# A second fold of the sequence DFT, and zero-padded column tiles for the last 64 keys, in a fused attention and Fourier-mixing kernel

## Chip, cores, metric

One core of one Trainium2 chip. The metric is the device time of one execution in microseconds (us); the medians below are over several runs. The profile of a kernel is one execution taken by the hardware profiler; its span is some 2 us shorter than the timed run.

## The reference

Threshold attention over 8 batches, 8 heads, 576 positions, 64 columns a head; its output, as (batch, 576, 512), is mixed by a two-dimensional DFT of which the real part is kept, and goes through a normalised two-layer network. All in fp32.

```python
scores = scale * np.matmul(q, k.transpose(0, 1, 3, 2))
thresh = np.max(scores, axis=-1, keepdims=True) - tau
scores = np.where(scores >= thresh, scores, -1e9)
attn = softmax(scores)                      # written out in the reference
x = heads_side_by_side(np.matmul(attn, v))  # (8, 576, 512)

X = np.fft.fft(np.fft.fft(x, axis=1), axis=2)
u = x + np.real(X)
un = (u - mean(u)) / np.sqrt(var(u) + 1e-6)
out = u + np.maximum(un @ w_ch1, 0.0) @ w_ch2   # 512 -> 2048 -> 512
```

## The kernel before

Heads go two at a time: 32 pairs, four to a batch, five query tiles to a pair. Every pair ends in `weighted_values`. Its last chunk of 64 keys is done in 64x64 tiles of the array. Then GpSimd folds x by the symmetry of the cosine and the sine, x(s) + x(576-s) and x(s) - x(576-s).

```python
    for c in range(4):
        for j in range(2):
            nc.tensor.matmul(pv[64*j : 64*j+64, 0:HALF], vt[:, 2*c+j, :],
                             e_t[:, 4*j+c, cols], start=(c == 0), stop=False, ...)
    for j in range(2):
        hp = slice(64 * j, 64 * j + 64)
        nc.tensor.matmul(pv[hp, 0:HALF], vt[hp, 8, :], ends[hp, 0, cols],
                         start=False, stop=True, ...)
    # ... x = pv times the reciprocal sums, on VectorE; then
    nc.gpsimd.tensor_copy(f[:, p, 0:KH:HALF], x[:, 0:KH:HALF])
    nc.gpsimd.tensor_tensor(out=f[:, p, 1:HALF], in0=up, in1=down, op=ALU.add)
    nc.gpsimd.tensor_tensor(out=f[:, p, KH:S], in0=up, in1=down, op=ALU.subtract)
```

After a batch's fourth pair its mixing starts: sums over the four pairs on VectorE (`s01` first), the DFT over the columns (`py`), and the DFT over the sequence, five calls of

```python
    def over_seq(y, table, rows, cols, m):
        pa = ps.tile([128, 512], FP32, tag="mm", name="pa")
        for u in range(3):                      # rows: 128, 128 and 33 or 31
            n = rows[u][1]
            nc.tensor.matmul(pa[0:m, 0:KH], y[0:n, u, cols], table[0:n, u, :],   # KH = 289
                             start=(u == 0), stop=(u == 2))
```

The network (`ph`, `po`) of earlier batches is woven between the attention steps of later ones. The order of instructions on each engine is fixed when the kernel is built, from estimated times: an engine that meets an instruction whose input is late stands still, whatever stands behind it.

Of the kernel before, what the change touches and what calls it, by code (L numbers as in the profile page):

```python
# [47 lines left out]
def kernel(  # L48
# [12 lines left out]
    nc = tc.nc  # L61
# [21 lines left out]
    ps = ctx.enter_context(tc.tile_pool(name="ps", bufs=2, space=bass.MemoryType.PSUM))  # L83


    loaded = {}
# [6 lines left out]
    def load_pair(n):  # L93
# [3 lines left out]
        kt = sb.tile([128, NT, 2, D], FP32, tag="k", bufs=1, name="k_in")  # L97
        vt = sb.tile([128, 9, D], FP32, tag="v", name="v_in")
        for j, h in enumerate(hs):
# [14 lines left out]
        nc.sync.dma_start(out=kt[64:128, 0:4, 1, :], in_=rows[:, 0])  # L114
        nc.sync.dma_start(out=kt[0:64, 1:5, 1, :], in_=rows[:, 1])

        for j, h in enumerate(hs):
            nc.sync.dma_start(
                out=vt[:, j:8:2, :], in_=v[b, h, 0:512, :].rearrange("(t p) d -> p t d", p=128)
            )  # L120
            nc.sync.dma_start(out=vt[64 * j : 64 * j + 64, 8, :], in_=v[b, h, 512:576, :])
        loaded[n] = (qt, kt, vt)

    load_pair(0)


# [30 lines left out]

    E_ROWS = [(0, 128), (128, 128), (256, KH - 256)]
    O_ROWS = [(0, 128), (128, 128), (256, HALF - 1 - 256)]
    seq_c = const.tile([128, 3, KH], FP32, name="seq_c")  # L160
    seq_s = const.tile([128, 3, KH], FP32, name="seq_s")
    for u in range(3):
        r, n = E_ROWS[u]
        nc.gpsimd.dma_start(out=seq_c[0:n, u, :], in_=dft_seq[r : r + n, 0:KH])
        r, n = O_ROWS[u]
        nc.gpsimd.dma_start(out=seq_s[0:n, u, :], in_=dft_seq[1 + r : 1 + r + n, KH : 2 * KH])

# [22 lines left out]

    load_dim()

    w1 = [const.tile([128, HID], FP32, name=f"w1_{c}") for c in range(ND)]
# [8 lines left out]
    u_t = const.tile([128, ND, RING], FP32, name="u_t")  # L202
    y_e = const.tile([128, 3, EH], FP32, name="y_e")
    y_o = const.tile([128, 3, 256], FP32, name="y_o")


# [78 lines left out]
    xs = {}  # L285
    folds = {}

    def prep_pair(n):

        qt, kt, vt = loaded.pop(n)  # L290
        ts = []
        for src, tag in ((qt, "qT"), (kt, "kT")):
            pt = ps.tile([128, 1024], FP32, tag="wide", bufs=3, name="pt")
            for t in range(NT):
                m = ROWS[t]
                nc.tensor.transpose(  # L296
                    pt[:, 128 * t : 128 * t + m], src[0:m, t, :, :], ident[0:m, 0:m]
                )
            dst = sb.tile([128, S], FP32, tag=tag, name=tag)
            if tag == "qT":  # L300
                nc.vector.tensor_scalar(
                    out=dst[:, :], in0=pt[:, 0:S], scalar1=q_scale[:, :], scalar2=None, op0=ALU.mult
                )
            else:
                nc.scalar.copy(dst[:, :], pt[:, 0:S])
            ts.append(dst)
        heads[n] = (ts[0], ts[1], vt)
        if n + 1 < B * NPAIR:
            load_pair(n + 1)
# [49 lines left out]
    def transposed_weights(i):  # L359
# [3 lines left out]
        if t == 0:  # L363
# [5 lines left out]
            if PAIRS[n % NPAIR] % 2:  # L369

                vt = sb.tile([128, 9, D], FP32, tag="vr", bufs=1, name="v_rev")
                src = heads[n][2]
# [23 lines left out]
    def weighted_values(n):  # L396
# [3 lines left out]
        if n % NPAIR == 0:  # L400
            xs[b] = [None] * NPAIR
            folds[b] = sb.tile([128, ND, S], FP32, tag="fold", bufs=1, name="fold")
        x = sb.tile([128, S], FP32, tag=f"x{p}", bufs=1, name=f"x{p}")
        for h in range(2):
            cols = slice(HALF * h, HALF * (h + 1))
            pv = ps.tile([128, 512], FP32, tag="mm", name="pv")
            for c in range(4):
                for j in range(2):
                    nc.tensor.matmul(  # L409
                        pv[64 * j : 64 * j + 64, 0:HALF], vt[:, 2 * c + j, :],  # L410
                        e_t[:, 4 * j + c, cols], start=(c == 0), stop=False,
                        skip_group_check=True,
                    )
            for j in range(2):
                hp = slice(64 * j, 64 * j + 64)
                nc.tensor.matmul(  # L416
                    pv[hp, 0:HALF], vt[hp, 8, :], ends[hp, 0, cols],
                    start=False, stop=True, skip_group_check=True,
                )
            nc.vector.tensor_tensor(  # L420
                out=x[:, cols], in0=pv[:, 0:HALF], in1=ends[:, 1, cols], op=ALU.mult
            )
        if p % 2:

            swap = sb.tile([2, S], FP32, tag="swap", bufs=1, name="swap")
            for j in range(2):
                nc.sync.dma_start(out=swap[j : j + 1, :], in_=x[64 * j : 64 * j + 1, :])
            for j in range(2):
                nc.sync.dma_start(out=x[64 * j : 64 * j + 1, :], in_=swap[1 - j : 2 - j, :])
        xs[b][p] = x  # L430
        up, down = x[:, 1:HALF], _reversed(x[:, HALF + 1 : S])
        f = folds[b]
        nc.gpsimd.tensor_copy(f[:, p, 0:KH:HALF], x[:, 0:KH:HALF])
        nc.gpsimd.tensor_tensor(out=f[:, p, 1:HALF], in0=up, in1=down, op=ALU.add)
        nc.gpsimd.tensor_tensor(out=f[:, p, KH:S], in0=up, in1=down, op=ALU.subtract)

    MIX = 4 * (3 * 5 * 128 + 5 * 3 * KH)

# [3 lines left out]
    def mixing(b):  # L442
        x = xs.pop(b)
        f = folds.pop(b)
        slot = slice(S * (b % 2), S * (b % 2) + S)



        E, O = slice(0, KH), slice(KH, S)
        s01 = sb.tile([128, 2, S], FP32, tag="tmp", bufs=1, name="s01")  # L450
        nc.vector.tensor_tensor(out=s01[:, :, :], in0=f[:, 0:2, :], in1=f[:, 2:4, :], op=ALU.add)
# [15 lines left out]
        SIN = ((0, 0, 128), (3, 128, 256))  # L467
        for u in range(3):
            for odd in range(2):
                r, n = (O_ROWS if odd else E_ROWS)[u]  # L470
                py = ps.tile([128, 512], FP32, tag="mm", name="py")
                table, first = (dim_s, 0) if odd else (dim_c, 1)
                for c, c0, c1 in SIN if odd else COS:
                    nc.tensor.matmul(  # L474
                        py[0:n, c0:c1], f[:, c, odd * KH + r : odd * KH + r + n],
                        table[:, c0:c1], start=True, stop=True, skip_group_check=True,
# [9 lines left out]

        def over_seq(y, table, rows, cols, m):
            pa = ps.tile([128, 512], FP32, tag="mm", name="pa")
            for u in range(3):
                n = rows[u][1]  # L490
                nc.tensor.matmul(  # L491
                    pa[0:m, 0:KH], y[0:n, u, cols], table[0:n, u, :],
                    start=(u == 0), stop=(u == 2),
                )
            return pa

        for t in range(2):
            cols = slice(128 * t, 128 * t + 128)
            tmp = sb.tile([128, 3, KH], FP32, tag="tmp", bufs=1, name="tmp")
            low, high, sin = (tmp[:, c, :] for c in range(3))  # L500
            pb = over_seq(y_o, seq_s, O_ROWS, cols, 128)
            nc.scalar.copy(sin, pb[:, 0:KH])
            yield MIX / 11
            pa = over_seq(y_e, seq_c, E_ROWS, cols, 128)

# [18 lines left out]
            if t == 1:  # L524

                pa = over_seq(y_e, seq_c, E_ROWS, slice(256, 257), 1)
                nc.scalar.copy(sin[0:1, :], pa[0:1, 0:KH])
# [100 lines left out]
    for i in range(total + 1):  # L628
# [9 lines left out]
        if i > 0 and t == 0:  # L638
            weighted_values(n - 1)
        for _ in itertools.islice(chunks, 2):  # L640
            pass
# [61 lines left out]
```

## Time and profile before

| | before |
|---|---|
| time, median of the first 3 runs | 1922.66 us (1922.33 to 1924.85) |
| TensorE busy | 96% of the span |
| VectorE, ScalarE, GpSimd busy | 45%, 32%, 12% |
| granted TensorE clock, mean | 0.973 |
| half-clock stretches after 250 us | none until the last microsecond |

The lines, and how they are read, stand with the prediction.

### The profile page before, as it was taken

To read this page: it belongs to the slowest core of one execution; us is meant where nothing else is said; L and a number is where in the kernel's file an instruction comes from. 1 tells how busy PE (TensorE), PEld (TensorE's weight loads), DVE (VectorE), ACT (ScalarE), POOL (GpSimd) and SP (SyncE) were. 2 spreads that over 40 slices of the span, in tenths; PEclk is the share of its full clock that TensorE was granted. 3 is DMA by queue.
4 is the path that set the end of the run, shared out by engine and by line. 5 is a ranking of instruction groups with operands and counts; after the bars stand their busy time and mean duration, and the time that the engine had idled before them with its cause. 6 is when DMAs were issued, how large, how long until landed. Compare 5 with 4: busy or idle time off the path is not lost.

```text
span 1923.0 us, 20963 instructions
## 1 busy us (share of the span) xinstructions
PE 1845.8 (96%) x7840; PEld 992.8 (52%) x7840; DVE 870.4 (45%) x2015; ACT 612.5 (32%) x1110; POOL 236.9 (12%) x438
## 2 busy tenths in 40 slices
PE   6777899999999999999999999999999999999999
PEld 3444555455455455545555455545545445545454
DVE  6998555534333544544334444544434355431010
ACT  3555434333123334323223234322323233421010
POOL 3433110110000110011000020002000020001000
PEclk8876899999999999999999999999999999999999
DMA  5432100100000110100000010101000001000000
GB/s 150 129 113 77 32 19 14 37 24 13 18 22 22 30 25 14 31 24 13 18 24 19 18 31 13 31 24 25 13 23 19 24 19 25 1 11 6 11 6 16
DMA packets 129701, 56.97 MB, mean 30 GB/s; under 512 B 120677, under 2 KB 120678, under 8 KB 129600
## 3 DMA queue, kind: packets, MB, share of 16 engines
q1 hardware_dynamic: 129232, 54.71, 10.5%
q8 instruction: 62, 1.02, 0.2%
q0 software_dynamic: 368, 0.93, 0.2%
q14 instruction: 39, 0.32, 0.1%
HBM read 46.02 MB, written 9.44 MB: 29 GB/s over the span
## 4 chain that ended last, share of the span: by engine, by line
PE 86%; DVE 9%; ACT 1%; POOL 1%; issue 1%; SPq 0%; DMA 0%; DVEq 0%; ACTq 0%
PE po L582 26%; PE ph L561 25%; PE sc L319 10%; PE pv L409 7%; PE pw L387 6%; PE pa L491 3%; PE pt L296 2%; PE pv L416 2%; DVE neg L332 2%; PE py L474 2%; DVE e L345 2%; DVE stage L241 1%; PE pe L392 1%; PE pe L393 1%; DVE w L229 1%
## 5 line engine op out<-in xcount | busy, mean ns | idle before, releaser
L582 PE MATMUL po<-w,h 128*128 128x512 f32 x1152 | 537.3, 603 | 0.0
L561 PE MATMUL ph<-u_t,w 128*128 128x384 f32 x1536 | 528.7, 493 | 5.4 <-DVE h L569 3.3
L342 ACT ACTIVATE e<-sc,neg 128x576 f32<-128x576 f32 (+1 forms) x320 | 229.3, 740 | 582.3 <-DVE neg L332 579.4
L561 PEld LDWEIGHTS ph<-u_t,w 128*128 128x128 f32 x1536 | 280.7, 190 | 207.3 <-issue 22.5
L332 DVE TENSOR_REDUCE neg<-sc 128x1 f32<-128x576 f32 (+1 forms) x320 | 229.8, 750 | 328.3 <-PE sc L319 328.0
L582 PEld LDWEIGHTS po<-w,h 128*128 128x128 f32 x1152 | 204.4, 190 | 229.8 <-issue 224.4
L319 PE MATMUL sc<-kT,qT 64*128 64x288 f32 (+1 forms) x1280 | 260.2, 450 | 36.3 <-ACT e_t L390 19.1
L345 DVE SCALAR_TENSOR_TENSOR e<-sc,thr,e 128x576 f32<-128x576 f32 (+1 forms) x320 | 250.9, 814 | 30.3 <-ACT e L342 13.0
L319 PEld LDWEIGHTS sc<-kT,qT 64*128 64x128 f32 (+1 forms) x1280 | 128.5, 183 | 168.3 <-issue 99.6
L390 ACT COPY e_t<-pw 128x1024 f32<-128x1024 f32 (+1 forms) x160 | 148.3, 927 | 160.1 <-PE pw L387 154.8
L354 POOL COPY rec<-den 128x128 f32<-128x128 f32 (+1 forms) x160 | 50.0, 313 | 1105.0 <-DVE den L352 933.8
L387 PEld LDWEIGHTS pw<-ident,e 128*128 128x128 f32 (+1 forms) x1280 | 141.7, 146 | 72.3 <-issue 55.5
L387 PE MATMUL pw<-ident,e 128*128 128x128 f32 (+1 forms) x1280 | 168.7, 275 | 0.1
L567 ACT ACTIVATE h<-ph 128x384 f32<-128x384 f32 x96 | 47.2, 492 | 314.7 <-PE ph L561 314.7
L569 DVE TENSOR_SCALAR h<-ph 128x384 f32<-128x384 f32 x96 | 53.4, 556 | 185.1 <-PE ph L561 184.9
L420 DVE TENSOR_TENSOR x<-pv,ends 128x288 f32<-128x288 f32 x64 | 29.3, 457 | 192.1 <-PE pv L416 175.3
L589 DVE SCALAR_TENSOR_TENSOR u<-po,rstd,u 128x512 f32<-128x512 f32 x36 | 27.0, 750 | 157.1 <-PE po L582 157.1
L409 PE MATMUL pv<-e_t,v_in 128*64 128x288 f32 x512 | 72.5, 420 | 0.0
L409 PE MATMUL pv<-e_t,v_rev 128*64 128x288 f32 x512 | 71.8, 420 | 0.3
L394 ACT COPY ends<-pe 128x256 f32<-128x256 f32 (+1 forms) x160 | 57.1, 357 | 3.2 <-PE pe L393 3.2
L409 PEld LDWEIGHTS pv<-e_t,v_in 128*64 128x64 f32 x512 | 35.0, 139 | 38.0 <-issue 10.8
L409 PEld LDWEIGHTS pv<-e_t,v_rev 128*64 128x64 f32 x512 | 34.8, 139 | 37.6 <-issue 11.6
(98 smaller groups left out, 1266.4 us busy)
## 6 DMA issues: line engine op xcount, KB each, us to landing
stage<-in_moe_w_ch_dram SPq DMA_DIRECT2D x32, 512.0 KB, 4.0
out_dram<-u SPq DMA_DIRECT2D x36, 256.0 KB, 2.0
q_in<-in_q_dram SPq DMA_DIRECT2D x64, 128.0 KB, 2.4
v_in<-in_v_dram SPq DMA_DIRECT2D x64, 128.0 KB, 2.3
k_in<-in_k_dram SPq DMA_DIRECT2D x32, 128.0 KB, 2.4
k_in<-in_k_dram SPq DMA_DIRECT2D x64, 64.0 KB, 2.3
q_in<-in_q_dram SPq DMA_DIRECT2D x64, 16.0 KB, 2.2
k_in<-in_k_dram SPq DMA_DIRECT2D x64, 16.0 KB, 2.1
```

Of the source, the lines that this page charges most:

```text
L319: nc.tensor.matmul(sc[j][0:m, c, 0:HALF], qT[hp, 128 * t : 128 * t + m], kT[hp, HALF * c : HALF * (c + 1)], start=True, stop=True,)
L332: nc.vector.tensor_reduce(out=neg[0:m, j : j + 1], in_=sc[j][0:m, :, 0:HALF], axis=AXIS_XY, op=ALU.max, negate=True,)
L342: nc.scalar.activation(out=ej, in_=sc[j][0:m, :, 0:HALF], func=ACT.Exp, bias=neg[0:m, j : j + 1], scale=1.0)
L345: nc.vector.scalar_tensor_tensor(out=ej, in0=sc[j][0:m, :, 0:HALF], scalar=thr[0:m, j : j + 1], in1=ej, op0=ALU.is_ge, op1=ALU.mult, accum ...
L387: nc.tensor.transpose(pw[:, 4 * j + c, 0:m], e[0:m, c0 : c0 + 128], ident[0:m, 0:m])
L390: nc.scalar.copy(e_t[:, :, qs], pw[:, :, 0:m])
L394: nc.scalar.copy(ends[:, :, qs], pe[:, 0:2, 0:m])
L409: nc.tensor.matmul(pv[64 * j : 64 * j + 64, 0:HALF], vt[:, 2 * c + j, :], e_t[:, 4 * j + c, cols], start=(c == 0), stop=False, skip_group_ ...
L491: nc.tensor.matmul(pa[0:m, 0:KH], y[0:n, u, cols], table[0:n, u, :], start=(u == 0), stop=(u == 2),)
L561: nc.tensor.matmul(ph[:, 0:GT], w1[c][:, 128 * j : 128 * (j + 1)], u_t[:, c, c0 : c0 + GT], start=(c == 0), stop=(c == ND - 1),)
L569: nc.vector.tensor_relu(ht, ph[:, 0:GT])
L582: nc.tensor.matmul(po[:, :], hT[j // 4][:, j % 4, 128 * t : 128 * (t + 1)], w2[j][:, :], start=(j == 0), stop=(j == NJ - 1),)
```

## The change

Its intent is less TensorE work. The folded sequence is folded again about its quarter: even frequencies need only one half-sum, odd ones the other. Each `over_seq` becomes four matmuls of 145 or 144 columns with full 128-row chunks, which write every second column of the PSUM tile. The last 64 keys become a fifth chunk of the same 128x64 column tiles, with v padded by zero rows.

```diff
-            for c in range(4):
+            for c in range(5):
                 for j in range(2):
                     nc.tensor.matmul(
                         pv[64 * j : 64 * j + 64, 0:HALF], vt[:, 2 * c + j, :],
-                        e_t[:, 4 * j + c, cols], start=(c == 0), stop=False,
+                        e_t[:, 4 * j + c, cols] if c < 4 else ends[:, 0, cols],
+                        start=(c == 0), stop=(c == 4), skip_group_check=True,
...
-        nc.gpsimd.tensor_copy(f[:, p, 0:KH:HALF], x[:, 0:KH:HALF])
-        nc.gpsimd.tensor_tensor(out=f[:, p, 1:HALF], in0=up, in1=down, op=ALU.add)
-        nc.gpsimd.tensor_tensor(out=f[:, p, KH:S], in0=up, in1=down, op=ALU.subtract)
+        for c, op in enumerate((ALU.add, ALU.subtract)):
+            nc.gpsimd.tensor_tensor(out=half[:, c, 1:HALF], in0=up, in1=down, op=op)
+        for c, c0, op in (
+            (0, 0, ALU.add), (0, 161, ALU.subtract), (1, FW, ALU.subtract), (1, FW + 161, ALU.add)
+        ):
+            nc.gpsimd.tensor_tensor(
+                out=f[:, p, c0 : c0 + mid - 1], in0=half[:, c, 1:mid],
+                in1=_reversed(half[:, c, mid + 1 : HALF]), op=op,
+            )
+        # ... and two sums of two columns each, on GpSimd
...
+        for parity, u, table, extra in ((0, 0, seq_even, seq_xe), (1, 2, seq_odd, seq_xo)):
+            at = pa[0:m, parity:KH:2]
+            nc.tensor.matmul(at, y[:, u, cols], table[:, odd, :], start=True, stop=False, ...)
+            nc.tensor.matmul(at, y[:, 1, cols], extra[:, odd, :], start=False, stop=True, ...)
...
     load_pair(0)
+    load_v(0)
+    load_v(1)
     # ... the sequence tables: raw rows through the buffers of tag "e", SyncE's queue,
     #     and strided copies on GpSimd, in place of six direct loads on GpSimd's queue
```

More of the change, by code (lines that the diff above doesn't have):

```diff
@@ L83 @@
     ps = ctx.enter_context(tc.tile_pool(name="ps", bufs=2, space=bass.MemoryType.PSUM))
+    y_e = const.tile([128, 3, EH], FP32, name="y_e")
+    y_o = const.tile([128, 3, 256], FP32, name="y_o")
+    FW = 304
+    f = const.tile([128, ND, 2 * FW], FP32, name="f")
+    nc.gpsimd.memset(f[:, :, :], 0.0)
+    nc.vector.memset(y_e[:, 1, :], 0.0)
+    nc.vector.memset(y_o[:, 1, :], 0.0)
+    v_in = [const.tile([128, 10, D], FP32, name=f"v_in{u}") for u in range(2)]
+    for u in range(2):
+        for j in range(2):
+            nc.gpsimd.memset(v_in[u][64 - 64 * j : 128 - 64 * j, 8 + j, :], 0.0)
     loaded = {}
@@ L97, in load_pair @@
         kt = sb.tile([128, NT, 2, D], FP32, tag="k", bufs=1, name="k_in")
-        vt = sb.tile([128, 9, D], FP32, tag="v", name="v_in")
         for j, h in enumerate(hs):
@@ L115, in load_pair, with load_v @@
         nc.sync.dma_start(out=kt[0:64, 1:5, 1, :], in_=rows[:, 1])
-        for j, h in enumerate(hs):
+        loaded[n] = (qt, kt)
+    def load_v(n):
+        b, p = n // NPAIR, PAIRS[n % NPAIR]
+        vt = v_in[n % 2]
+        for j in range(2):
+            h = 2 * p + (j + p) % 2
             nc.sync.dma_start(
@@ L120, in load_pair @@
             )
-            nc.sync.dma_start(out=vt[64 * j : 64 * j + 64, 8, :], in_=v[b, h, 512:576, :])
-        loaded[n] = (qt, kt, vt)
+            nc.sync.dma_start(out=vt[64 * j : 64 * j + 64, 8 + j, :], in_=v[b, h, 512:576, :])
     load_pair(0)
+    load_v(0)
+    load_v(1)
     ident = const.tile([128, 128], FP32, name="ident")
@@ L154, with load_seq @@
     nc.vector.tensor_tensor(out=thr_off[:], in0=tau_pos[:], in1=below[:], op=ALU.add)
-    E_ROWS = [(0, 128), (128, 128), (256, KH - 256)]
-    O_ROWS = [(0, 128), (128, 128), (256, HALF - 1 - 256)]
-    seq_c = const.tile([128, 3, KH], FP32, name="seq_c")
-    seq_s = const.tile([128, 3, KH], FP32, name="seq_s")
-    for u in range(3):
-        r, n = E_ROWS[u]
-        nc.gpsimd.dma_start(out=seq_c[0:n, u, :], in_=dft_seq[r : r + n, 0:KH])
-        r, n = O_ROWS[u]
-        nc.gpsimd.dma_start(out=seq_s[0:n, u, :], in_=dft_seq[1 + r : 1 + r + n, KH : 2 * KH])
+    NE, NO = KH // 2 + 1, KH // 2
+    seq_even = const.tile([128, 2, NE], FP32, name="seq_even")
+    seq_odd = const.tile([128, 2, NO], FP32, name="seq_odd")
+    seq_xe = const.tile([128, 2, NE], FP32, name="seq_xe")
+    seq_xo = const.tile([128, 2, NO], FP32, name="seq_xo")
+    def load_seq():
+        nc.gpsimd.memset(seq_xe[:, :, :], 0.0)
+        nc.gpsimd.memset(seq_xo[:, :, :], 0.0)
+        for pieces, dst, parity, parts in (
+            (((0, 1, 128),), seq_even, 0, ((0, 128),)),
+            (((0, 16, 128),), seq_odd, 1, ((0, 128),)),
+            (((0, 129, 16), (16, 0, 1)), seq_xe, 0, ((0, 17),)),
+            (((32, 0, 16),), seq_xo, 1, ((32, 16),)),
+        ):
+            raw = sb.tile([128, 2 * KH], FP32, tag="e", name="seq_raw")
+            for p, r, n in pieces:
+                nc.sync.dma_start(out=raw[p : p + n, :], in_=dft_seq[r : r + n, :])
+            if dst is seq_xo:
+                nc.sync.dma_start(out=raw[32:33, KH : 2 * KH], in_=dft_seq[144:145, KH : 2 * KH])
+            for p, n in parts:
+                for c in range(2):
+                    nc.gpsimd.tensor_copy(
+                        dst[p : p + n, c, :], raw[p : p + n, KH * c + parity : KH * (c + 1) : 2]
+                    )
     dim_c = const.tile([128, 1 + 256], FP32, name="dim_c")
@@ L191 @@
     load_dim()
+    load_seq()
     w1 = [const.tile([128, HID], FP32, name=f"w1_{c}") for c in range(ND)]
@@ L202 @@
     u_t = const.tile([128, ND, RING], FP32, name="u_t")
-    y_e = const.tile([128, 3, EH], FP32, name="y_e")
-    y_o = const.tile([128, 3, 256], FP32, name="y_o")
     ones = const.tile([128, 128], FP32, name="ones")
@@ L285 @@
     xs = {}
-    folds = {}
     def prep_pair(n):
-        qt, kt, vt = loaded.pop(n)
+        qt, kt = loaded.pop(n)
         ts = []
@@ L306, in prep_pair @@
             ts.append(dst)
-        heads[n] = (ts[0], ts[1], vt)
+        heads[n] = (ts[0], ts[1], v_in[n % 2])
         if n + 1 < B * NPAIR:
@@ L369, in transposed_weights @@
             if PAIRS[n % NPAIR] % 2:
-                vt = sb.tile([128, 9, D], FP32, tag="vr", bufs=1, name="v_rev")
+                vt = sb.tile([128, 10, D], FP32, tag="vr", bufs=1, name="v_rev")
                 src = heads[n][2]
@@ L401, in weighted_values @@
             xs[b] = [None] * NPAIR
-            folds[b] = sb.tile([128, ND, S], FP32, tag="fold", bufs=1, name="fold")
         x = sb.tile([128, S], FP32, tag=f"x{p}", bufs=1, name=f"x{p}")
@@ L410, in weighted_values @@
                         pv[64 * j : 64 * j + 64, 0:HALF], vt[:, 2 * c + j, :],
-                        e_t[:, 4 * j + c, cols], start=(c == 0), stop=False,
-                        skip_group_check=True,
-                    )
-            for j in range(2):
-                hp = slice(64 * j, 64 * j + 64)
-                nc.tensor.matmul(
-                    pv[hp, 0:HALF], vt[hp, 8, :], ends[hp, 0, cols],
-                    start=False, stop=True, skip_group_check=True,
-                )
+                        e_t[:, 4 * j + c, cols] if c < 4 else ends[:, 0, cols],
+                        start=(c == 0), stop=(c == 4), skip_group_check=True,
+                    )
             nc.vector.tensor_tensor(
@@ L423, in weighted_values @@
         if p % 2:
-            swap = sb.tile([2, S], FP32, tag="swap", bufs=1, name="swap")
+            swap = sb.tile([2, S], FP32, tag="half", bufs=1, name="swap")
             for j in range(2):
@@ L430, in weighted_values @@
         xs[b][p] = x
+        half = sb.tile([128, 2, HALF], FP32, tag="half", bufs=1, name="half")
         up, down = x[:, 1:HALF], _reversed(x[:, HALF + 1 : S])
-        f = folds[b]
-        nc.gpsimd.tensor_copy(f[:, p, 0:KH:HALF], x[:, 0:KH:HALF])
-        nc.gpsimd.tensor_tensor(out=f[:, p, 1:HALF], in0=up, in1=down, op=ALU.add)
-        nc.gpsimd.tensor_tensor(out=f[:, p, KH:S], in0=up, in1=down, op=ALU.subtract)
-    MIX = 4 * (3 * 5 * 128 + 5 * 3 * KH)
+        mid = S // 4
+        for c, op in enumerate((ALU.add, ALU.subtract)):
+            nc.gpsimd.tensor_tensor(out=half[:, c, 1:HALF], in0=up, in1=down, op=op)
+        for c, c0, op in (
+            (0, 0, ALU.add), (0, 161, ALU.subtract), (1, FW, ALU.subtract), (1, FW + 161, ALU.add)
+        ):
+            nc.gpsimd.tensor_tensor(
+                out=f[:, p, c0 : c0 + mid - 1], in0=half[:, c, 1:mid],
+                in1=_reversed(half[:, c, mid + 1 : HALF]), op=op,
+            )
+        nc.gpsimd.tensor_tensor(
+            out=f[:, p, mid - 1 : mid + 1], in0=_stepped(x, mid, -mid, 2),
+            in1=_stepped(x, 3 * mid, -mid, 2), op=ALU.add,
+        )
+        nc.gpsimd.tensor_tensor(
+            out=_stepped(f[:, p, :], 160, FW, 2), in0=_stepped(x, 0, mid, 2),
+            in1=_stepped(x, HALF, mid, 2), op=ALU.subtract,
+        )
+    MIX = 4 * (3 * 5 * 128 + 5 * 2 * KH)
     def mixing(b):
         x = xs.pop(b)
-        f = folds.pop(b)
         slot = slice(S * (b % 2), S * (b % 2) + S)
-        E, O = slice(0, KH), slice(KH, S)
-        s01 = sb.tile([128, 2, S], FP32, tag="tmp", bufs=1, name="s01")
+        E, O = slice(0, FW), slice(FW, 2 * FW)
+        s01 = sb.tile([128, 2, 2 * FW], FP32, tag="tmp", bufs=1, name="s01")
         nc.vector.tensor_tensor(out=s01[:, :, :], in0=f[:, 0:2, :], in1=f[:, 2:4, :], op=ALU.add)
@@ L467, in mixing @@
         SIN = ((0, 0, 128), (3, 128, 256))
-        for u in range(3):
+        for u, r, n in ((0, 0, 128), (1, 128, 48), (2, 176, 128)):
             for odd in range(2):
-                r, n = (O_ROWS if odd else E_ROWS)[u]
                 py = ps.tile([128, 512], FP32, tag="mm", name="py")
@@ L474, in mixing @@
                     nc.tensor.matmul(
-                        py[0:n, c0:c1], f[:, c, odd * KH + r : odd * KH + r + n],
+                        py[0:n, c0:c1], f[:, c, odd * FW + r : odd * FW + r + n],
                         table[:, c0:c1], start=True, stop=True, skip_group_check=True,
@@ L485, in mixing, with over_seq @@
                 yield MIX / 11
-        def over_seq(y, table, rows, cols, m):
+        def over_seq(y, odd, cols, m):
             pa = ps.tile([128, 512], FP32, tag="mm", name="pa")
-            for u in range(3):
-                n = rows[u][1]
+            for parity, u, table, extra in ((0, 0, seq_even, seq_xe), (1, 2, seq_odd, seq_xo)):
+                at = pa[0:m, parity:KH:2]
                 nc.tensor.matmul(
-                    pa[0:m, 0:KH], y[0:n, u, cols], table[0:n, u, :],
-                    start=(u == 0), stop=(u == 2),
+                    at, y[:, u, cols], table[:, odd, :], start=True, stop=False,
+                    skip_group_check=True,
+                )
+                nc.tensor.matmul(
+                    at, y[:, 1, cols], extra[:, odd, :], start=False, stop=True,
+                    skip_group_check=True,
                 )
@@ L500, in mixing @@
             low, high, sin = (tmp[:, c, :] for c in range(3))
-            pb = over_seq(y_o, seq_s, O_ROWS, cols, 128)
+            pb = over_seq(y_o, 1, cols, 128)
             nc.scalar.copy(sin, pb[:, 0:KH])
             yield MIX / 11
-            pa = over_seq(y_e, seq_c, E_ROWS, cols, 128)
+            pa = over_seq(y_e, 0, cols, 128)
             nc.vector.tensor_tensor(out=low, in0=pa[:, 0:KH], in1=sin, op=ALU.subtract)
@@ L524, in mixing @@
             if t == 1:
-                pa = over_seq(y_e, seq_c, E_ROWS, slice(256, 257), 1)
+                pa = over_seq(y_e, 0, slice(256, 257), 1)
                 nc.scalar.copy(sin[0:1, :], pa[0:1, 0:KH])
@@ L639 @@
             weighted_values(n - 1)
+            if n + 1 < B * NPAIR:
+                load_v(n + 1)
         for _ in itertools.islice(chunks, 2):
```

## The prediction

> **What bounds the kernel now.** I read the page's busy table and forty slices first, then the table by stage, then the groups of the lines that the diff touches, then the order of time around single uses of them. The busy table, the slices and the chain of work that ended last:
>
> ```profile
> PE 1845.8 (96%) x7840; PEld 992.8 (52%) x7840; DVE 870.4 (45%) x2015; ACT 612.5 (32%) x1110; POOL 236.9 (12%) x438
> ...
> PE   6777899999999999999999999999999999999999
> ...
> DVE  6998555534333544544334444544434355431010
> ...
> PE 86%; DVE 9%; ACT 1%; POOL 1%; issue 1%; SPq 0%; DMA 0%; DVEq 0%; ACTq 0%
> ```
>
> The table by stage (PE, PEld, DVE, ACT, POOL busy, then granted clock, DMA share, GB/s):
>
> ```profile
> 100.00:150.00 50.00, 37.76 (x149) 21.01 (x149) 45.41 (x92) 25.16 (x42) 18.50 (x18) 0.70 0.35 113
> 600.00:1000.00 400.00, 395.65 (x1739) 210.28 (x1738) 175.43 (x413) 126.74 (x226) 41.31 (x87) 1.00 0.09 23
> ```
>
> There are two stages. From about 250 us to the end TensorE is busy 99% at full clock while VectorE is at 44%: here time saved in the matmul stream is time saved in the end. In the first 200 us the weights are converted; VectorE is the bound (45 of 50 us), TensorE waits and its clock is partly halved; matmul time saved there is worth nothing, and delays of the first loads count.
>
> A busy time is a union of overlapping records, so I take the cost of matmuls from start to start. One fp32 matmul is two records (1152 records for 576 calls at L582); a record is called a pass here. In the order of time, one sequence-DFT sum and what follows it, then one pair's weighted values:
>
> ```profile
> 661.73 1.92 PE L491 MATMUL pa<-seq_c,y_e 128*128 128x289 f32 x6
> ...
> 662.90 0.29 PEld L491 LDWEIGHTS pa<-seq_c,y_e 33*128 33x128 f32 x2 [0.39 <-issue]
> ...
> 663.58 0.55 PE L387 MATMUL pw<-ident,e 128*128 128x128 f32 x3
> ```
>
> ```profile
> 1016.07 2.16 PE L409 MATMUL pv<-e_t,v_in 128*64 128x288 f32 x16
> 1018.16 0.70 PE L416 MATMUL pv<-ends,v_in 64*64 64x288 f32 x4
> 1018.80 2.16 PE L409 MATMUL pv<-e_t,v_in 128*64 128x288 f32 x16
> 1020.89 0.70 PE L416 MATMUL pv<-ends,v_in 64*64 64x288 f32 x4
> 1021.52 5.43 PE L561 MATMUL ph<-u_t,w 128*128 128x384 f32 x16
> ```
>
> The sum takes 663.58 - 661.73 = 1.85 us; the pair takes 1021.52 - 1016.07 = 5.45 us. Read singly, passes in the steady part start 0.246 us apart at 289 columns, 0.243 at 288 (two column tiles together), 0.109 at 128 (transposes): 0.84 ns a column plus some 2 ns. On top stand the changes of shape: the last pass before the 33-row chunk is 0.335 to the next start instead of 0.246, the first one after it 0.347, and the same again leaving it. A first pass of a group costs some 0.1 more, because its weight load is not hidden.
>
> **What the Trainium skill says.** (1) "TensorEngine Tiling (Array Packing)", Key Properties: a change of tiling mode drains TensorE, a change of tile within a mode doesn't. The trace agrees: weight loads of the 33-row chunk sit 0.39 us idle and the starts spread by 0.09 to 0.10 on each side; so does the 64x64 remainder of the weighted values. (2) "TensorE: Matmul & The Clock Gate", LDWEIGHTS: the time goes with the columns of the weights, not with the rows. The trace agrees: 184 ns for 33x128, 190 for 128x128. So zero padding of the rows is free. (3) "PSUM — Partial Sum Buffer", Specifications: lines are 8 bytes and a non-contiguous pattern slows matmuls significantly. The new sums write every second fp32 column. No matmul of the kernel before does, so its trace can't say. (4) "GPSIMD Engine Reference", side-by-side cycle accounting: about 2.6 cycles an element for two-input work. The trace has 800 ns for 287 elements and 0.75 us from start to start, some 2.1 ns an element (2.6 cycles at that page's 1.2 GHz): it agrees.
>
> **The change part by part.**
>
> *Sequence DFT (L491).* Before: 3 chunks x 2 passes x 289 columns, with two shape changes, 1.85 us; four a batch, and a fifth with one output row (6 passes at 0.244 plus changes, 1.64 us from 671.39 to 673.03). A batch is 4 x 1.85 + 1.64 = 9.04 us, eight batches 72 us. After: 4 matmuls x 2 passes x 145 or 144 columns, all of 128 rows. A pass is 145 x 0.84 + 2 = 0.124 us if columns still set it. Weight loads don't: in the 65-column passes at L474, where loads must bind, 128-column weights follow each other every 0.111 us. So 8 x 0.124 + 0.10 = 1.09 us, and about 1.08 for the single row: 5.45 us a batch, 44 us in all. **Saved: 28 us**, two thirds from fewer columns, the rest from shape changes. It is all in the TensorE-bound stage (the first use is at 226 us).
>
> *Last 64 keys.* Before: each half has 8 tile pairs, then two more pairs in 64x64 mode, 2.72 us. After: 10 pairs in one mode. A pair of tiles of 288 columns takes 0.243, so a whole head pair takes 20 x 0.243 + some 0.15 of entry and exit = 5.0 us against 5.45. **Saved 0.45 x 32 = 14 us**, less the first batch's four pairs, which lie in the VectorE-bound stage: 12.6 us.
>
> *First DFT (L474).* Same 15 matmuls and same copies; the small chunk is 48 wide instead of 33/31 and comes second. Nothing.
>
> *Folding on GpSimd.* Before, a pair is one small copy and two sums of 287: first start 640.36 to end 642.05, 1.7 us. After, two sums of 287 (0.75 each), four of 143 (0.14 + 143 x 2.1 ns = 0.44 each) and two tiny ones: 3.6 us. GpSimd goes from 237 to about 300 us busy and stays far from a bound, but for the last pair of a batch the fold is on the path: VectorE's first sum of the mixing waits for it. Behind that sum, in VectorE's queue, stand the maxima of the scores:
>
> ```profile
> 640.36 0.19 POOL L433 COPY fold<-x 128x2 f32<-128x2 f32 x1 [9.20 <-DVE x L420]
> ...
> 642.08 1.36 DVE L451 TENSOR_TENSOR s<-fold 128x1152 f32<-128x1152 f32 x1 [1.78 <-POOL fold L435]
> ...
> 645.84 0.75 PE L319 MATMUL sc<-kT,qT 64*128 64x288 f32 x2 [1.15 <-ACT e_t L390]
> ```
>
> TensorE already stands still for 1.15 to 1.3 us there in most batches. If the order of instructions stays, nearly 1.9 us more come on top eight times, 15 us; if more matmuls are put ahead, nothing. I take **+10 us**. VectorE's folded sums are 608 wide instead of 576, 1 us in all: included.
>
> *Start.* Six table loads leave the GpSimd queue, but the new raw tables go through the queue of SyncE and through the two buffers named "e", which the dim table and then the first scores' exponentials use too. That is a chain: dim table copied out on VectorE, then a raw table in, two copies, the next one in; an issue lands in about 3.5 us. Second, tau is loaded behind four more transfers of v, at about 0.6 us each: VectorE's first useful work waits 10.5 us for tau now, and would wait some 2.4 more. The first exponential starts at 15.7 us now and would start at 20 to 25. Part of this VectorE can fill with weights. I take **+6 us** (0 to 12), and nothing back later, because this stage is bound by VectorE.
>
> Sum: -28 - 12.6 + 10 + 6 = -25 us, that is 1922.7 - 25 = 1898 us.
>
> **The rivals.** *A: the strided write costs.* If a column on its own 8-byte line doubles a pass, 8 x 0.246 + 0.10 = 2.07 us stand against 1.85: 83 us in all, 11 us lost instead of 28 gained, and the end is at 1937. For it: the skill's sentence. Against it: an fp32 pass delivers a column only every 0.84 ns, twice the 0.42 ns that one column a cycle at 2.4 GHz would need, so the write port should have time for one line each; the transposes show the same 0.84. I give A three in ten. *B: TensorE's saving turns into waiting.* The shorter stream hits the fold chain at each mixing, and the first 250 us grow more: then +20 and +12 and the end is near 1914. For it: GpSimd's doubled fold and the shared buffers. Against it: TensorE has other matmuls for most of the time. *C: everything is hidden* (fold and start cost nothing): 1882, just faster by 2%. For it: forty slices full of work that can move; against: in-order queues, seen standing still above.
>
> **Range and chances.** Seven in ten for the free write, centred on 1898 with some 10 us either way; three in ten for 1937. The middle of this mixture is a little above the first centre: 1902 us. The range 1886 to 1940 should hold it 8 times in 10. Faster by over 2% (below 1884) needs C: 0.11. Slower by over 2% (above 1961) needs A and a bad start: 0.04. Within 2%: 0.85.
>
> **What would show it.** Passes at the sum's line 0.124 us apart (free) or 0.25 (A), a sum 1.09 or 2.07 us. Ten pairs of tiles in one mode per half, 0.243 apart, and no 64x64 form in that group. GpSimd's fold of a pair 3.6 us, and idle time of TensorE just after the eight first sums of the mixing, 1.2 us now, 2 to 3 then. The first exponential at 20 to 25 us and the slice 200:250 later by about 6 us. The prediction is wrong if strided passes take over 0.25, if the schedule at the mixing's start is quite another, or if the weights' stage moves by more than 12 us.

## The result

The changed kernel takes 1926.64 us (median of 4 runs, 1925.53 to 1927.05) against 1923.76 for the kernel before (4 runs): a ratio of 1.001, 95% interval 0.9991 to 1.0029, so the same time. Ratios here are the mean time of one kernel's fast runs over that of the other's of the same rounds, so not quite the ratio of the medians. The predicted 1902 us was a gain of 20 us; nothing of it was there, though the time lies in the stated range.

The changed kernel's busy table, its slices of the granted clock, and its chain of work that ended last:

```profile
PE 1825.5 (95%) x7920; PEld 1021.3 (53%) x7920; DVE 872.4 (45%) x2017; ACT 611.2 (32%) x1110; POOL 304.3 (16%) x607
...
PEclk9876799999999999999999999999999999999999
...
PE 85%; DVE 9%; POOL 3%; ACT 1%; issue 1%; DVEq 0%; ACTq 0%; POOLq 0%
```

TensorE has 20 us less busy time in a span that is 2 us longer. GpSimd, 1% of the chain before, is 3% of it. The clock's slices look full after the sixth; each is 48 us long, and a few us at half speed don't show in its tenths. The matmuls themselves became just what was forecast. One pair's weighted values and one sequence sum in the order of time of the changed kernel:

```profile
1021.23 2.16 PE L448 MATMUL pv<-e_t,v_in 128*64 128x288 f32 x16
1023.22 0.66 PE L448 MATMUL pv<-ends,v_in 128*64 128x288 f32 x4
1023.71 2.11 PE L448 MATMUL pv<-e_t,v_in 128*64 128x288 f32 x16
...
1026.23 2.85 PE L613 MATMUL ph<-u_t,w 128*128 128x384 f32 x8
```

```profile
667.24 0.52 PE L539 MATMUL pa<-seq_even,y_e 128*128 128x145 f32 x2
667.60 0.41 PE L543 MATMUL pa<-seq_xe,y_e 128*128 128x145 f32 x2
667.84 0.41 PE L539 MATMUL pa<-seq_odd,y_e 128*128 128x144 f32 x2
668.09 0.41 PE L543 MATMUL pa<-seq_xo,y_e 128*128 128x144 f32 x2
668.33 1.04 PE L427 MATMUL pw<-ident,e 128*128 128x128 f32 x8
```

The pair takes 1026.23 - 1021.23 = 5.00 us, as forecast (5.45 before); the sum 668.33 - 667.24 = 1.09, as forecast (1.85 before). Added up from start to start after 250 us, without the waits between them, the weighted values fell from 152.5 to 142.1 us and the sequence sums from 62.2 to 38.1: 34 us were saved there.

They were lost again at the starts of the mixings. The order of time at one of them:

```profile
642.03 1.54 POOL L469 TENSOR_TENSOR half<-x 128x287 f32<-128x287 f32 x2 [8.96 <-DVE x L453]
...
643.53 1.82 POOL L473 TENSOR_TENSOR f<-half 128x143 f32<-128x143 f32 x4
...
645.71 1.43 DVE L500 TENSOR_TENSOR s<-f 128x1216 f32<-128x1216 f32 x1 [3.75 <-POOL f L482]
647.05 0.75 DVE L372 TENSOR_REDUCE neg<-sc 128x1 f32<-128x576 f32 x1
...
648.47 1.00 ACT L430 COPY e_t<-pw 128x1024 f32<-128x1024 f32 x1
...
649.53 1.52 PE L359 MATMUL sc<-kT,qT 64*128 64x288 f32 x4 [3.21 <-ACT e_t L430]
```

Read it upwards. TensorE stood still 3.21 us for a PSUM buffer that ScalarE had to empty (`e_t`); ScalarE's queue stood behind the exponential of the next scores, which needs their maximum; VectorE's maximum stood in its queue behind `s`, the mixing's first sum; and `s` waited 3.75 us for GpSimd's fold, which runs from 642.03 to 645.7, 3.7 us. Before, that wait was 1.78 us and TensorE's stall 1.15. At every second mixing (385, 831 and 1278 us) the stall, 3.22 us, stands before the mixing's own first DFT (`py`), which waits for the same sums on VectorE; before it was 1.29. What follows the stall is in the table by stage (PE, PEld, DVE, ACT, POOL busy, granted clock, DMA share, GB/s), here cut around it:

```profile
646.00:650.30 4.30, 1.09 (x4) 0.66 (x4) 4.30 (x6) 2.11 (x3) 0.00 (x0) 1.00 0.00 0
650.30:657.10 6.80, 6.80 (x17) 3.94 (x17) 4.21 (x12) 1.06 (x4) 0.29 (x1) 0.50 0.00 0
657.10:662.00 4.90, 4.88 (x27) 2.83 (x26) 2.48 (x6) 3.34 (x8) 0.00 (x0) 0.99 0.01 3
```

TensorE works again and is fully busy, but for 6.8 us its granted clock is 0.50. The same place before has 1.00 throughout. After 250 us the changed kernel has 34 us at half clock (seven stretches, all but one at a mixing), the kernel before none until its last microsecond, and TensorE's idle time from 250 to 1885 us went from 17.4 to 35.7 us. Of these 18 us, 14 stand at the seven mixings' starts (stalls of 7.7 us in all, then 21.8).

### The profile page after: what moved, and what is told of

Same layout as the page of the kernel before. It is cut to its first block, busy times and chain, and to the rows that moved or that the text cites. A ratio compares the mean times of both kernels' runs of the same rounds, so it can differ in the third digit from the quotient of the medians.

```text
span 1925.3 us, 21347 instructions
## 1 busy us (share of the span) xinstructions
PE 1825.5 (95%) x7920; PEld 1021.3 (53%) x7920; DVE 872.4 (45%) x2017; ACT 611.2 (32%) x1110; POOL 304.3 (16%) x607
## 4 chain that ended last, share of the span: by engine, by line
PE 85%; DVE 9%; POOL 3%; ACT 1%; issue 1%; DVEq 0%; ACTq 0%; POOLq 0%
PE po L634 26%; PE ph L613 25%; PE sc L359 11%; PE pv L448 8%; PE pw L427 6%; PE pt L336 2%; PE py L522 2%; DVE neg L372 2%; DVE e L385 1%; PE pa L539 1%; DVE stage L282 1%; PE pa L543 1%; POOL f L473 1%; PE pe L432 1%; PE pe L433 1%
## 5 line engine op out<-in xcount | busy, mean ns | idle before, releaser
L359 PE MATMUL sc<-kT,qT 64*128 64x288 f32 (+1 forms) x1280 | 266.9, 453 | 47.0 <-ACT e_t L430 26.2
L359 PEld LDWEIGHTS sc<-kT,qT 64*128 64x128 f32 (+1 forms) x1280 | 132.7, 184 | 177.4 <-issue 92.6
L430 ACT COPY e_t<-pw 128x1024 f32<-128x1024 f32 (+1 forms) x160 | 148.0, 925 | 152.5 <-PE pw L427 146.8
L469 POOL TENSOR_TENSOR half<-x 128x287 f32<-128x287 f32 x64 | 50.8, 815 | 146.1 <-DVE x L453 124.8
L473 POOL TENSOR_TENSOR f<-half 128x143 f32<-128x143 f32 x128 | 60.9, 505 | 0.0
```

What stands on the lines that cost most here:

```text
L359: nc.tensor.matmul(sc[j][0:m, c, 0:HALF], qT[hp, 128 * t : 128 * t + m], kT[hp, HALF * c : HALF * (c + 1)], start=True, stop=True,)
L430: nc.scalar.copy(e_t[:, :, qs], pw[:, :, 0:m])
L473: nc.gpsimd.tensor_tensor(out=f[:, p, c0 : c0 + mid - 1], in0=half[:, c, 1:mid], in1=_reversed(half[:, c, mid + 1 : HALF]), op=op,)
```

## The experiments

The theory: both parts save on TensorE what the passes say; the longer GpSimd fold makes each stall at a mixing some 2 us longer; and a stall of that length makes the throttle halve the clock, which costs as much again. Rivals: a denser stream is itself what the throttle answers to; late folds are covered by other matmuls, so that the cause is elsewhere; the strided write costs; or the order of instructions alone made the difference.

### The column tiles alone: pv_only

```diff
 # on the kernel before: five chunks of column tiles, v in two padded constant buffers, load_v as changed
```

> The kernel before with the zero-padded column tiles for the last 64 keys alone. Theory (the stream gains are real; the longer GpSimd fold at each mixing, and the clock it drops, ate them): the fold is as before, so TensorE's stall at a mixing stays 1.2 us and the clock stays full after 250 us; ten tile pairs per half, 0.243 us apart, no shape change: 12 us saved, 2 lost at the start because tau is loaded behind four more transfers: 1912 to 1914 us. Rival (a denser TensorE stream is itself what the throttle answers, by power): the clock drops in this kernel too, and the time stays at 1921 to 1925.

Measured: 1911.08 us against 1922.97, ratio 0.9944 (0.993 to 0.9957). The stalls at the mixings stayed at 1.17 to 1.32 us, with one half-clock stretch of 3.4 us after 250 us. The theory holds: this part brings its 11 to 12 us when the fold is left alone. The denser stream alone did not lower the clock: the runs' means are 0.974 to 0.977, those of the kernel before 0.972 to 0.978.

### The second fold alone: seq_only

```diff
 # on the changed kernel
-            for c in range(5):
+            for c in range(4):
 ...
+            for j in range(2):
+                hp = slice(64 * j, 64 * j + 64)
+                nc.tensor.matmul(pv[hp, 0:HALF], vt[hp, 8 + j, :], ends[hp, 0, cols],
+                                 start=False, stop=True, skip_group_check=True)
```

> The changed kernel with the old 64x64 tiles for the last 64 keys, so the second fold of the sequence DFT alone. Theory: sums cost 1.09 us instead of 1.85 (23 us saved), but the GpSimd fold is 3.7 us long, the stall at seven mixings is 3.2 us (14 us more) and half-clock windows follow (some 15 us more), 2 us at the start: 1930 to 1938 us, slower than both. Rival (the two parts together make the stream too dense): this part alone shows its gain, 1901 to 1908 us, with the clock full after 250 us.

Measured: 1939.54 us against 1922.97, ratio 1.0089 (1.0075 to 1.0103): slower than both, 1.5 us above the upper end of what was expected. The stalls are 3.2 us, and 48 us after 250 us are at half clock. So the second fold as it stands costs 17 us net, and the column tiles pay most of it back. The two parts' separate effects, -12 and +17, sum to the +3 of the result to within 2 us.

### The cost of a late fold, measured by itself: delay1, delay2, delay3

These have nothing of the change. On the kernel before, GpSimd does one, two or three extra sums of 287 columns into a scratch tile at the last fold of a batch. The edit puts them before the fold, but the kernel is scheduled anew, and the traces show where they run: the first before the fold, the second inside it, the third after it.

```diff
+        if n % NPAIR == NPAIR - 1:
+            scratch = sb.tile([128, S], FP32, tag="swap", bufs=1, name="scratch")
+            for _ in range(3):           # 1, 2, 3
+                nc.gpsimd.tensor_tensor(out=scratch[:, 0:287], in0=up, in1=down, op=ALU.add)
```

> The kernel before with one sum of 287 columns (0.75 us, nobody reads it) on GpSimd ahead of the last pair's fold. Theory: the stall at seven mixings goes from 1.2 to about 2.0 us, 5 us in all; the clock is halved at some of them, since windows fell into stalls of 1.4 to 1.7 us in some runs and not in others: 1928 to 1940 us, with a wide spread from run to run. Rival (the clock answers only to stalls near 3.2 us): 1927 to 1930 with a spread as before.

> The same with two such sums (1.5 us). Theory: stalls of about 2.7 us, 10.5 us in all, and a half-clock window at most of the mixings, some 12 to 16 us: 1940 to 1948 us, a step below the 1948 with three sums. Rival (the clock answers only to stalls near 3.2 us): 1932 to 1936.

> The kernel before, with three sums of 287 columns into a scratch tile (0.75 us each, nobody reads them) put on GpSimd ahead of the fold of the last pair of a batch: 2.25 us of delay at eight places and nothing else of the change. Theory: the stall at a mixing goes from 1.2 to about 3.4 us and brings half-clock windows with it: 16 us of stall and some 15 of clock, 1950 to 1958 us. Rival (a late fold is covered by other matmuls): under 1930 us.

The stall at the same mixing with one, two and three such sums, from the orders of time of the three kernels; for two and three also the fold's last sum on GpSimd and the sum `s` that waits for it:

```profile
644.13 0.75 PE L319 MATMUL sc<-kT,qT 64*128 64x288 f32 x2 [1.90 <-ACT e_t L390]
```

```profile
642.39 0.79 POOL L439 TENSOR_TENSOR fold<-x 128x287 f32<-128x287 f32 x1
643.22 1.36 DVE L455 TENSOR_TENSOR s<-fold 128x1152 f32<-128x1152 f32 x1 [3.28 <-POOL fold L439]
...
646.97 1.24 PE L319 MATMUL sc<-kT,qT 64*128 64x288 f32 x4 [2.65 <-ACT e_t L390]
```

```profile
643.65 0.79 POOL L439 TENSOR_TENSOR fold<-x 128x287 f32<-128x287 f32 x1
...
644.40 0.79 POOL L436 TENSOR_TENSOR scratch<-x 128x287 f32<-128x287 f32 x1
644.48 1.93 DVE L455 TENSOR_TENSOR s<-fold 128x1152 f32<-128x1152 f32 x1 [3.29 <-POOL fold L439]
...
648.81 2.29 PE L319 MATMUL sc<-kT,qT 64*128 64x288 f32 x4 [3.22 <-ACT e_t L390]
```

Measured: 1934.08, 1941.31 and 1948.33 us against 1923.97 (the first two) and 1922.97; ratios 1.0064 (1.005 to 1.0077), 1.0096 (1.0084 to 1.0109) and 1.0134 (1.012 to 1.0148). The steps cost about 10, then 7 and 8 us. The third sum did not make the fold later (`s` waits 3.29 us as against 3.28), but while it ran beside `s`, `s` took 1.93 us instead of 1.36. From the end of VectorE's last x to the end of `s` it is 3.14 us before, 3.89, 4.64 and 5.22 with one, two and three sums, and 5.18 in the changed kernel. The cost is more than the stalls themselves: the idle time after 250 us rose by 4.7, 9.4 and 13.3 us. The rest goes with the half-clock stretches, which are 20.5, 27.3 and 34.1 us long. So delay3 makes `s` end 2.08 us later, by luck almost what the change does (2.04), and with stalls as long (3.22 us) it loses 25 us without the change. Of those 2.08 us 1.5 are a late fold and the rest a slower `s`; delay1 and delay2 are late folds alone. The third run came out 2 us below what was expected. The order of instructions shifts a little in these kernels too, since the kernel is scheduled anew.

### The fold shortened in place: short_fold (wrong result)

```diff
-        ):
+        )[0 : 0 if n % NPAIR == NPAIR - 1 else 4]:   # the four sums of 143 left out for the last pair
```

> The changed kernel with a wrong result on purpose: the last pair of each batch does not do its four sums of 143 columns (1.9 us on GpSimd), and nothing else is changed; the fold stays on GpSimd. Theory (the length of that fold is the cause): the stall at a mixing is back at 1.2 to 1.5 us, the clock stays full after 250 us, and 14 us of stalls and some 17 of clock come back: 1892 to 1898 us. Rival (moving the fold helped only because it changed the order of instructions): 1915 us or more.

Measured: 1904.76 us (1893.71 to 1909.70, 6 runs) against 1923.09, ratio 0.9889 (0.9864 to 0.9915). Some 22 us of the changed kernel's time go with those four sums, with the fold still on GpSimd; that speaks against the rival of order alone, though the order shifts a little here too. But the median is 7 us above what was expected, and the spread of 16 us is the widest. The trace says why: the stalls did not come down to 1.2 us but to 1.43 (three) and 1.66 (three), and the clock was halved at each of the longer ones and at none of the shorter ones. The runs' mean granted clock points the same way, if loosely, since it holds the start too: 0.972 and 0.977 in the two fastest runs, 0.965, 0.970 and 0.972 in the three slowest. Two more stretches lie elsewhere, after a stall of 0.89 us (at 1607 us) and at the last mixing. That 1.43 us passed here and 1.66 did not is no fixed edge: a stall of 1.18 us brought a stretch in pv_only.

### The last fold on VectorE: fold_dve, and the same for the kernel before: before_dve

```diff
+        last = n % NPAIR == NPAIR - 1
+        other = nc.vector if last else nc.gpsimd
-            nc.gpsimd.tensor_tensor(out=half[:, c, 1:HALF], in0=up, in1=down, op=op)
+            other.tensor_tensor(out=half[:, c, 1:HALF], in0=up, in1=down, op=op)
 # and the same for the four sums of 143 and the two of two columns
```

> The changed kernel with the fold of the last head pair of each batch on VectorE instead of GpSimd; the other three pairs as they were. Theory: VectorE needs some 2.3 us for it where GpSimd needs 3.7, so the scores' maxima behind the first mixing sum come earlier, TensorE's stall falls from 3.2 to about 1.8 us and no longer reaches the length at which the clock is halved: 10 us of stalls and some 15 of clock come back, 1900 to 1904 us. Rival (the clock falls for another reason, or the stall has another cause): within 5 us of the changed kernel, 1921 to 1929.

The order of time at the same mixing, fold on VectorE:

```profile
637.82 0.83 DVE L471 TENSOR_TENSOR half<-x 128x287 f32<-128x287 f32 x2
...
639.69 1.43 DVE L504 TENSOR_TENSOR s<-f 128x1216 f32<-128x1216 f32 x1
...
640.52 1.01 ACT L430 COPY e_t<-pw 128x1024 f32<-128x1024 f32 x1 [10.80 <-PE pw L427]
...
642.08 1.23 PE L359 MATMUL sc<-kT,qT 64*128 64x288 f32 x4
```

Measured: 1889.99 us against 1922.97, ratio 0.9828 (0.9814 to 0.9842). That is better than expected by 10 us, and the lines show it: the fold takes 1.9 us (637.82 to 639.69) instead of 3.7, but in this build ScalarE also empties `e_t` before the exponential, so TensorE does not stand still at all here (0.40 us at every second mixing), where 1.8 us were expected. Two causes then, the shorter fold and an order that came with it; this run can't part them. Idle time after 250 us is 15.7 us, and one stretch of 3.4 us is at half clock.

> The kernel before with the fold of the last pair of each batch on VectorE, as in the run that reached 1890 us. Theory: the stalls before were 1.2 us and left the clock alone, so only these can be won: 8 us at most, 1914 to 1921 us, and the rest of the distance to 1890 is the change's own. Rival (moving the fold would have brought 33 us to any kernel): 1888 to 1895 us.

Measured: 1912.63 us against 1923.09, ratio 0.995 (0.9939 to 0.9962). Stalls fell to 0.33 and 0.47 us. This is 1 us better than the expected range and far from 1890. With the stall out of the way on both sides, the change is worth 1912.6 - 1890.0 = 23 us. As it was made, it was worth nothing.

### Contiguous writes: contig (wrong result)

```diff
-            at = pa[0:m, parity:KH:2]
+            at = pa[0:m, 145 * parity : 145 * parity + (NO if parity else NE)]
```

> The changed kernel with a wrong result on purpose: the sequence sums write the even and odd frequencies as two contiguous runs of 145 and 144 columns in place of every second column. Theory (a stride of two fp32 columns costs an fp32 pass nothing): passes stay at 0.123 us and the time within 4 us of the changed kernel, 1922 to 1930. Rival (part of the missing gain is in the strided write): passes below 0.12 us and a time under 1918.

The same sum in the order of time, columns now contiguous:

```profile
666.75 0.52 PE L539 MATMUL pa<-seq_even,y_e 128*128 128x145 f32 x2
667.11 0.41 PE L543 MATMUL pa<-seq_xe,y_e 128*128 128x145 f32 x2
667.35 0.41 PE L539 MATMUL pa<-seq_odd,y_e 128*128 128x144 f32 x2
667.60 0.41 PE L543 MATMUL pa<-seq_xo,y_e 128*128 128x144 f32 x2
667.84 0.82 PE L427 MATMUL pw<-ident,e 128*128 128x128 f32 x6
```

667.84 - 666.75 = 1.09 us, as with the stride. The time, 1929.11 us (ratio 1.0033 to the kernel before), is no better than the changed kernel's. The stride costs nothing here.

### The start as well: best

On fold_dve, v of the second pair is loaded after the first pair's transposes are issued, and the sequence tables are loaded in slot 17, through buffers that the weights have left.

```diff
-    load_v(1)
 ...
-    load_seq()                     # raw rows in tag "e"
+        if i == 17:
+            load_seq()             # raw rows in tags h0 to h3
```

> The changed kernel with the last fold on VectorE, and the start put right: the second pair's v is loaded after tau, and the sequence tables are loaded in slot 17 through the weights' staging buffers instead of the exponentials' buffers. Theory: the first exponential is back at 15.7 us or earlier (18.85 in the changed kernel) and the lag of some 3 us at the first pair is gone: 1885 to 1888 us against 1890. Rival (the start's lag is taken up by VectorE's queue later anyway, or differs by chance from run to run): 1889 to 1892.

The weights' last step (the product on GpSimd) in the changed kernel and in this one, from the view by line:

```profile
L286 POOL TENSOR_TENSOR w<-w,stage x32: 1257/1344/1733, 33.1 to 182.3; 128x512 f32<-128x512 f32 x32
```

```profile
L284 POOL TENSOR_TENSOR w<-w,stage x32: 1256/1326/1735, 20.6 to 176.2; 128x512 f32<-128x512 f32 x32
```

Measured: 1885.51 us against 1923.09, ratio 0.9804 (0.9792 to 0.9817); correct, and the fastest of all; whether by more than 2% is unclear. The first weight product starts 12 us earlier than in the changed kernel and the last one 6 us earlier, and the time is 4.5 us below fold_dve's. The expectation named the wrong sign: the first exponential of scores came at 19.3 us, not 15.7, because weights went ahead of it. So what cost time at the start was, by these traces, not the late exponential but the late weights. pv_only, where v goes ahead of tau but the sequence tables load as before, says the same: its first exponential is at 18.96 us, its last weight product at 175.2, and its fourth pair's values come at 201.9 us (207.0 in the kernel before). So the late weights seem to go with the new loads of the sequence tables.

### The sums

From the traces, after 250 us (idle time to 1885 us) against the kernel before; "start" is the lag of the fourth pair's values at 207 us. All in us.

| run | matmuls saved | idle more | start | profile's span | left over | half clock | share |
|---|---|---|---|---|---|---|---|
| changed | -34.5 | +18.2 | +2.4 | +2.3 | 16.2 | 34.1 | 0.47 |
| seq_only | -22.1 | +18.2 | +0.6 | +16.3 | 19.6 | 47.8 | 0.41 |
| delay1 | 0 | +4.7 | -3.6 | +9.5 | 8.4 | 20.5 | 0.41 |
| delay2 | 0 | +9.4 | -2.3 | +16.3 | 9.2 | 27.3 | 0.34 |
| delay3 | 0 | +13.3 | -4.3 | +22.0 | 13.0 | 34.1 | 0.38 |

"Left over" is the span's difference less the three terms before it. Over five kernels it is 0.34 to 0.47 of the half-clock time. Half the speed can cost at most half of such a stretch, and part of a stretch is no matmul work, so this fits. It is a remainder, but the traces also have the clock's cost directly. One long stall of the changed kernel (3.22 us, ended at 385.40) was followed by full clock, and the next 100 passes took 21.82 us; the same 100 passes after the stalls at 831.02 and 1278.06, as long but with a half-clock stretch of 3.41 us behind them, took 23.46. So such a stretch cost 1.64 us, 0.48 of its length, and 34 us of them some 16.

What stays open: the starts of kernels with the same opening instructions differ by some 4 us between executions. Five traces with the start of the kernel before (before, before_dve, the three delays) begin the last weight product at 175.2 to 179.8 us, five with the changed start (changed, seq_only, short_fold, fold_dve, contig) at 182.2 to 182.8; their fourth pair's values come at 202.1 to 207.0 and at 206.9 to 209.8. So the start costs some 5 us on average. One half-clock stretch of the changed kernel, at 1176 us, follows a stall of only 0.9 us, as one does in seq_only, contig, short_fold and best, and why was not tested.

## Why the prediction was wrong

- **What bounds the kernel:** right. Less matmul time after 250 us is less time, wherever no stall eats it (pv_only).
- **Sequence DFT, 28 us:** the single sum was right to the digit, 1.09 us, and the strided write is free (contig). Added up after 250 us, for seven batches, 24.1 us were saved; that is 27.5 for eight. The term was right.
- **Last 64 keys, 12.6 us:** right; 10.4 us in the changed kernel's trace, 12 alone.
- **Folding on GpSimd, +10 us: this is the step that failed.** Its mechanism was named, and its 1.9 us was right (3.7 us against 1.7, stalls of 1.15 to 1.3 grown to 3.2). But its 15 us for the case that the order of instructions stays was then cut to 10 on the hope of a kinder order. The order stayed: the stalls at seven mixings grew by 14.1 us. And the term has a second half that the sum does not hold at all: a stall of that length mostly brings half-clock stretches, here 34 us of them, worth some 16 us. So the fold cost about 30 us instead of 10. (Another 4 us of idle time that nobody forecast came with the change: three waits of 0.9 us for `u_t` from GpSimd and one of 1.7 us at the last mixing.) delay3 shows the cost without the change, short_fold shows it go away.
- **Start, +6 us:** some 5, so about right, but through the weights, which were loaded later. Tau and the first exponential, the sign that the prediction named, cost nothing in pv_only; and the first exponential came at 18.85 us, not at 20 to 25.
- **Rival B** (saving turned into waiting) was the right one of the three, and named GpSimd's fold; its "+20 and +12" put 12 us on the start that belonged to the clock. **Rival A**, three chances in ten, fell: it drew the range up to 1940, and that the result lies inside the range while the mechanism was missed is luck.
- **Of the four places in the Trainium skill** three held in the changed kernel: the drains at changes of shape (their time was won back), the free padding of rows, GpSimd's rate for two inputs. The sentence on non-contiguous PSUM patterns did not (contig).

## What to carry to other kernels

Before work is moved from a saturated engine to an idle one, follow the idle engine's result to its first reader and see what stands behind that reader in its queue: here 2 us on an engine that was 12% busy cancelled 34 us of matmuls. Count a longer stall of TensorE again for the clock that may fall after it: of 39 stalls of 1.66 us and more at mixings 33 brought a half-clock stretch, of 15 shorter ones one did. And look at the granted clock around stalls, not at its mean, which moved only from 0.973 to 0.968.

## What the Trainium skill lacked or had wrong

- "TensorE: Matmul & The Clock Gate", Part 1 and the table of goals, asks for no TensorE gaps over some 3 to 3.4 us. Here far shorter stalls brought the half clock: at mixings after 250 us (the last one of each kernel left out) none of six with 1.15 to 1.29 us (before), one of six with 1.17 to 1.32 (pv_only), none of three with 1.43 and three of three with 1.66 us (short_fold), four of six with 1.9 to 2.04 (delay1), four of six with 2.65 to 2.68 (delay2), five of six with 3.2 in the changed kernel and in seq_only, six of six in contig and delay3. In each run the stretches start on one grid of 3.41 us. The six stalls of 1.9 us and more that brought none were all cut by a line of this grid (3.22 us at 385.40 into 1.92 and 1.30), with at most 1.92 us in one cell; each of the 25 cells (250 to 1700 us) with 2.1 us or more of idle time was followed by half clock. That the stretches come in multiples of 3.41 us (3.4, 6.8, 10.2) agrees with the page's window.
- "PSUM — Partial Sum Buffer", Specifications, says that any non-contiguous pattern slows matmuls significantly. With fp32 operands and every second fp32 column written, two passes of 145 columns took 0.245 us, and the four matmuls of a sum 1.09 us, the same as with contiguous columns.
- "TensorEngine Tiling (Array Packing)", Key Properties, says that a change of tiling mode drains TensorE but gives no cost. Here a 33-row chunk among 128-row ones made three passes start their successor 0.335, 0.347 and 0.334 us later instead of 0.246, and ten column-tile pairs in place of eight and two 64x64 ones saved 0.45 us per pair of heads.
